# Attention with a gated product and a sparse expert layer: second products three steps behind the first, and announcements of jumps to TensorE alone

## The chip, the cores and the metric

The kernel runs on one core of a Trainium2 chip. The metric is the device time of one execution in microseconds (us); the median of three runs is given. One execution is also recorded by the hardware profiler, and all rows come from that record. The engines are TensorE (PE, matrix products; PEld is its weight load), VectorE (DVE), ScalarE (ACT), GpSimd (POOL) and SyncE (SP, which only issues DMAs here). Each has its own instruction stream; they meet in semaphores.

## The reference

```
# 1: attention, 8 batches, S = 1856, D = 256, 64 score columns
scores = z @ z.T / S;  attn = max(scores, 0) ** 2
x = (u * (attn @ v)).reshape(14848, 256)
# 2: experts, 4 groups of 4, F = 1024
g_idx = argmax(x @ w_group);  e_idx = argmax(xg @ w_expert[g])
h = max(xg @ w1[g, e], 0);  ye = h @ w2[g, e]
out[token] = (softmax weight of group and expert) * ye
```

All in float32. Each of the 14848 rows goes to one of 16 experts.

## The kernel before, in words

**Precision.** Every float32 operand of a product is split into a high and a low part (`hh` and `hl`, `xh` and `xl`, weights `h` and `l`), and a product is three matmuls: low by high, high by high, high by low. The high part is a copy on ScalarE, the low part a subtraction on VectorE.

**Two stages.** Up to about 858 us the attention runs, batch by batch; its result rows are routed and scattered into a bucket in DRAM, sorted by expert. Then comes the expert stage, which the change is about. The experts are ordered by their number of rows. Each has a list of blocks of rows (`PARTS`): 512 + 256 + 512 for the two largest, 384 + 256 + 512 for three more, 512 + 512 for eight, 384 + 512 for two, 512 + 352 for the last. The very first blocks of the two largest are done ahead.

**Steps.** A block takes NF = 8 steps, and `g` counts the steps of all blocks. `body(g)` issues, in this order: `up`, the first product of step g (six matmuls, L767 to L769, into one PSUM bank `ph`; ScalarE reads the bank into `hh`, L771; VectorE reads it into `hl`, L772, after which the bank is free); then `downs(g - AHEAD)`, the second product of an earlier step (six matmuls, L782 to L784, into the two banks `y` of its block); then, at three steps of a block, a piece of `join_block` for the next block (`xf`, `xh`, `xl`); then whatever `then(g, ...)` has put down for this step. Three banks serve `ph` in turn, four serve `y`, and one (`ps_m`) serves the router's small products.

**What hangs on a step.** After the last second product of a block, `turn` copies `y` to `yp` (ScalarE, L812), transposes it by DMA from SyncE into `yr` (L821), and some steps later `rows_out` makes `yf` on VectorE (a copy L827 and a multiply L831 for each half of the block) and scatters it to the output from POOL (L787). Weights come as four pieces of 512 KB an expert: SyncE loads a raw piece (`load_w`, L197, L206) one expert ahead of its cutting, and the cutting (ScalarE L201, L213; VectorE L202, L214) is put on the steps listed in `CUTS`, counted from the end of a region. A piece's next raw load is issued by the main loop after the step that cut it (`owed`). Rows of a coming block are transposed in by SyncE as `xp` (L728), from `more_rows`.

**Versions.** The last block of an expert has a number of rows known only at run time. It is compiled in eight versions, 512 to 288 columns wide; `region(i)` holds them. Each engine jumps by itself into the version that a register names, and jumps out at its end. A version holds the eight steps of its block and the first AHEAD steps of the next. `hint(j, engines)` issues an instruction that announces the coming jump's target to an engine: to TensorE right after the region before, to the other four in step 4 or 5 of the block ahead. There are fifteen such entries. The widths that the record shows, in order: 288, 288, 384, 384, 384, 512, 480, 448, 416, 416, 384, 352, 352, 480, 416. The first five follow a block of 256 rows, the others one of 512 or 384.

**Order.** In the expert stage the order on PE, ACT, DVE and SP is the program's order, as written (`manual_schedule`). An engine that waits holds up everything behind it.

Of the kernel before, what the change touches and what calls it, by code (L numbers as in the profile page):

```python
# [9 lines left out]
F32 = mybir.dt.float32  # L10
# [9 lines left out]
P = 128  # L20
# [11 lines left out]
def tile_glu_attn_moe(  # L32
# [14 lines left out]
    NE, _, F = w1.shape  # L47
    N = B * S
    ND = D // P
# [30 lines left out]
    ps_s = ctx.enter_context(tc.tile_pool(name="ps_s", bufs=3, space=PSUM))  # L80
    ps_o = ctx.enter_context(tc.tile_pool(name="ps_o", bufs=4, space=PSUM))
    ps_m = ctx.enter_context(tc.tile_pool(name="ps_m", bufs=1, space=PSUM))

    def sb(tag, shape, dt, bufs, name):
        return pool.tile(shape, dt, tag=tag, bufs=bufs, name=name)
# [7 lines left out]
    def new_stg(name):  # L93
        return sb("stg", [P, 1024], F32, 2, name)
# [4 lines left out]
    def new_rows(name):  # L99
        return sb("rows", [P, 4, RW], I32, 3, name)  # L100
# [7 lines left out]
    def bank(pl, tag, name):  # L108
        return pl.tile([P, 512], F32, tag=tag, name=name)
# [80 lines left out]
    def load_w(e, wt, piece, name, wide=False):  # L190

        if wide and piece > 1:
            raw = sb("ut", [P, ND, 512], F32, 2, f"raw_{name}_{piece}").rearrange("p d q -> p (d q)")
        else:
            raw = new_stg(f"raw_{name}_{piece}")
        if piece < 2:
            nc.sync.dma_start(raw, w1[ds(e, 1), piece * P:(piece + 1) * P, :].rearrange("o p f -> p (o f)"))  # L197

            def split():
                hi, lo = wt["h"][piece], wt["l"][piece]  # L200
                held(nc.scalar.copy(out=hi, in_=raw))  # L201
                nc.vector.tensor_sub(out=lo, in0=raw, in1=f32(hi))  # L202
        else:
            q = piece - 2
            rv = raw.rearrange("p (a d) -> p a d", d=D)
            nc.sync.dma_start(  # L206
                rv, w2[ds(e, 1), q * 4 * P:(q + 1) * 4 * P, :].rearrange("o (a p) d -> p (o a) d", p=P)
            )

            def split():  # L210
                for j in range(2):
                    t = wt["2"][2 * q + j].rearrange("p (a t d) -> p a t d", a=2, t=2)
                    held(nc.scalar.copy(out=t[:, :, 0, :], in_=rv[:, 2 * j:2 * j + 2, :]))  # L213
                    nc.vector.tensor_sub(out=t[:, :, 1, :], in0=rv[:, 2 * j:2 * j + 2, :], in1=f32(t[:, :, 0, :]))  # L214

        return split
# [123 lines left out]
    ut = {}  # L340
# [362 lines left out]
    dyn = {i for i in range(NB) if blocks[i] == parts[blocks[i][0]][-1] and blocks[i][0] < NDYN}  # L703
# [49 lines left out]
    def join_block(i, given=None):  # L753
# [5 lines left out]
        )  # L759
        yield from join_x(i, xp, n, given)  # L760

    def up(name, wt, x, f, W, given=None):
        xh, xl = x
        fs = slice(f * P, (f + 1) * P)
        o = bank(ps_s, "s", f"ph_{name}_{f}")[:, 0:W]
        for d in range(ND):
            nc.tensor.matmul(o, wt["l"][d][:, fs], xh[:, d, 0:W], start=(d == 0), stop=False)  # L767
            nc.tensor.matmul(o, wt["h"][d][:, fs], xh[:, d, 0:W], start=False, stop=False)  # L768
            nc.tensor.matmul(o, wt["h"][d][:, fs], xl[:, d, 0:W], start=False, stop=(d == ND - 1))  # L769
        hh, hl_ = given or (new_z(f"hh_{name}_{f}"), new_z(f"hl_{name}_{f}"))  # L770
        nc.scalar.activation(out=hh[:, 0:W], in_=o, func=AF.Relu)  # L771
        nc.vector.scalar_tensor_tensor(out=hl_[:, 0:W], in0=o, scalar=0.0, in1=f32(hh[:, 0:W]),  # L772
                                       op0=ALU.max, op1=ALU.subtract)
        return hh, hl_
# [84 lines left out]
    def next_view():  # L859
# [3 lines left out]
    PE, ACT, DVE, SP, POOL = (  # L863
        mybir.EngineType.PE, mybir.EngineType.Activation, mybir.EngineType.DVE, mybir.EngineType.SP, mybir.EngineType.Pool
    )
# [243 lines left out]
        nc.vector.tensor_copy(out=ki, in_=tiles)  # L1109


    AHEAD = 2
    OLD = NB - 1
    xb = {0: xs[0]}
    hb = {}
# [3 lines left out]
    def then(g, fn):  # L1119
        at.setdefault(g, []).append(fn)  # L1120

    CUTS = {2: (0, 6, 9, 13), 3: (0, 4, 6, 9), 4: (0, 2, 4, 8), 5: (0, 2, 4, 8)}
    cuts = {}
    owed = []

# [5 lines left out]
    def weights_from(g):  # L1131

        ld = blocks[g // NF - 1][0] + 2
        if ld >= NE:
            return
        wts[ld].update(new_w(f"e{ld}"))

        def piece(pc):
            cuts[(ld, pc)]()
            owed.append((ld + 1, pc))  # L1140

        for pc, k in enumerate(CUTS.get(ld, (0, 1, 3, 4))):
            then(g + k, lambda pc=pc: piece(pc))

    def downs(g, W=None):
        i, f = divmod(g, NF)
        e, r0, n = blocks[i]
        if f == 0 and i not in yb:
            yb[i] = [bank(ps_o, "o", f"y_{i}_{d}") for d in range(ND)]
        down(wts[e], f, hb.pop(g), yb[i], W or n)  # L1150
        if f == NF - 1:
            fns = turn(i, yb.pop(i), rows_b.pop(i)[1], n, W, ygiven.get(i))
            for k, fn in enumerate(fns):
                then(g + AHEAD + (5 if i in dyn else 8 if i == OLD - 1 else 6) + k, fn)

    ygiven = {}

# [38 lines left out]
    def body(g, W=None, given=None, xgiven=None):  # L1196

        i, f = divmod(g, NF)
        e, r0, n = blocks[i]
        d = (g - AHEAD) // NF  # L1200
        hb[g] = up(i, wts[e], xb[i], f, W if W and i in dyn else n, given)
# [13 lines left out]
    def hint(j, engines):  # L1215
        if j < NDYN:
            tc.switch_hint({eng: to_arm[j] for eng in engines}, NW, f"arm{j}")

    def region(i):

        g0 = i * NF
        yb[i] = [bank(ps_o, "o", f"y_{i}_{d}") for d in range(ND)]
        xgiven = new_xhl(f"m{i + 1}")
        ygiven[i] = [sb("zr", [P, 512], F32, 2, f"yr_{i}_{t0}") for t0 in (0, 2)]
        given = {
            g0 + NF + k: tuple(sb(tag, [P, 512], F32R, n, f"{h}_{i + 1}_{k}") for h in ("hh", "hl"))
            for k, (tag, n) in enumerate((("zm", 2), ("r", 4)))
        }
        held_state = [(x, dict(x)) for x in (hb, yb, xb, rows_b)]
        held_at = {k: list(v) for k, v in at.items()}  # L1230
        views_at = ocnt[0]
        owed_at = list(owed)
        for k in tc.Switch(to_arm[blocks[i][0]], NW, hint=f"arm{blocks[i][0]}"):
            for x, was in held_state:
                x.clear()
                x.update(was)
            at.clear()
            at.update({k_: list(v_) for k_, v_ in held_at.items()})
            ocnt[0] = views_at
            owed[:] = owed_at  # L1240
            for g in range(g0, g0 + NF + AHEAD):
                body(g, WIDE[k], given.get(g), xgiven)
                if g == g0 + NF - 1:
                    del xb[i]
        late["joined"] += 1
# [9 lines left out]
    with order:  # L1255
        g = 0
        while g < NB * NF:
            i, f = divmod(g, NF)
            e, r0, n = blocks[i]
            if f == 0 and i in dyn:  # L1260
                region(i)
                g += NF + AHEAD
                hint(e + 1, (PE,))
                weights_from(g)
                while owed:
                    load_piece(*owed.pop(0))
                more_rows()
                continue
            body(g)
            if i < NEARLY:  # L1270
                early(i)
            if i + 1 == NEARLY and f == 3:
                while deferred or gens:
                    early(i)
                more_rows()
                counts()
                arms()
                overflow_count()
            if i == NEARLY and f == 0:
                for pc in range(4):  # L1280
                    load_piece(NEARLY, pc)
                load_arms()
                hint(0, (PE,))
            while owed:
                load_piece(*owed.pop(0))
            if i + 1 in dyn and f == (4 if n < 3 * P else 5):
                hint(e, (ACT, DVE, SP, POOL))
            if i + 1 < NB and f == (4 if i + 1 == NEARLY else 3) + 2:
                late["joined"] += 1
            if f > 5:  # L1290
                more_rows()
            if f == NF - 1:
                del xb[i]
            g += 1
        after = [fn for k in sorted(at) for fn in at.pop(k)]
        i = NB - 1
        e, r0, n = blocks[i]
        hs = [hb.pop(i * NF + k) for k in range(NF)]
        with tc.manual_schedule(engines={POOL}):
            for fn in after:  # L1300
                fn()
            for t in range((n + P - 1) // P):
                rows_down(i, wts[e], hs, rows_b[i][1], n, t, next_view)
            assert not hb
            overflow()
# [36 lines left out]
```

## Time and profile before

| | us |
|---|---|
| median of three runs (1573.93 to 1580.88) | 1574.33 |
| the profiled execution | 1587.49 |
| its span, first to last instruction | 1585.7 |
| expert stage in it | about 858 to 1577 |
| TensorE busy in the span | 1514.5 |

The profiled execution is 13 us slower than the median; sums over its rows are made against its own 1587.49 us. "Issue" in the chain of waits or ahead of an instruction is time in which an engine waited for nothing that the profile shows; right behind a jump it is the time until the first instruction of the target is there. PEclk is the share of TensorE's clock that was granted.

### The profile page before, as it was taken

What the parts mean: (1) busy time and instruction counts of PE and PEld (TensorE: products, weight loads), DVE (VectorE), ACT (ScalarE), POOL (GpSimd) and SP (SyncE); (2) the same over time, 40 slices, a digit from 0 to 9 for tenths busy, and PEclk for the clock granted to TensorE, in tenths of its full rate; (3) what the DMA queues carried; (4) which work ended last, traced back from release to release, by engine and by line L of the source; (5) the groups of instructions that cost most, each with busy time, mean ns of one, the idle gap of its engine ahead of it and who ended that gap; (6) DMA issues with size and microseconds to landing.
All of it is one profiled execution on the core that took longest, in us unless ns stands there. A gap on an engine that the chain in (4) does not pass through costs nothing.

```text
span 1585.7 us, 24254 instructions
## 1 busy us (share of the span) xinstructions
PE 1514.5 (96%) x7607; PEld 1318.1 (83%) x7607; DVE 1103.6 (70%) x2619; ACT 996.1 (63%) x1885; POOL 297.0 (19%) x343
## 2 busy tenths in 40 slices
PE   9999999999999999999999999999999889889897
PEld 7888888888888888888887888998887778788796
DVE  7788888888787888887986565555555555555463
ACT  8888888888878888887873343444433334343342
POOL 0022121121212121111121212221122122122122
PEclk9999999999999999999999999999999999999999
DMA  5324333333344352325744646664565665455541
GB/s 142 100 82 106 83 82 105 77 105 85 75 101 92 78 113 68 89 70 151 235 116 90 136 105 131 141 121 93 101 123 117 126 122 115 79 117 119 107 84 48
DMA packets 303588, 167.76 MB, mean 106 GB/s; under 512 B 239467, under 2 KB 282477, under 8 KB 303216
## 3 DMA queue, kind: packets, MB, share of 16 engines
q1 hardware_dynamic: 290896, 132.63, 38.5%
q0 software_dynamic: 11968, 30.91, 7.1%
q14 instruction: 277, 2.27, 0.6%
q8 instruction: 95, 1.56, 0.4%
q10 hardware_dynamic: 352, 0.39, 0.1%
HBM read 72.51 MB, written 41.60 MB: 72 GB/s over the span
## 4 chain that ended last, share of the span: by engine, by line
PE 74%; issue 11%; DVE 6%; DMA 3%; ACT 2%; SPq 1%; POOL 1%; DVEq 0%; POOLq 0%; ACTq 0%
PE o L381 12%; PE o L382 12%; PE o L384 11%; PE sc L349 6%; PE sc L350 6%; PE y L784 5%; PE ph L767 4%; PE ph L768 4%; PE ph L769 4%; PE y L782 4%; PE y L783 4%; DVE hl L772 1%; DMA out_dram<-yf,meta 1%; DMA yr<-yp 1%; DVE w_e L214 1%
## 5 line engine op out<-in xcount | busy, mean ns | idle before, releaser
L771 ACT ACTIVATE hh<-ph 128x512 fp32r<-128x512 f32 (+7 forms) x296 | 151.4, 516 | 409.2 <-PE ph L769 345.1
L772 DVE SCALAR_TENSOR_TENSOR hl<-ph,hh 128x512 fp32r<-128x512 f32 (+7 forms) x296 | 169.8, 582 | 310.3 <-ACT hh L771 230.4
L381 PE MATMUL o<-ah,vl 128*128 128x512 f32 (+1 forms) x960 | 354.7, 371 | 0.8 <-DVE ah L359 0.4
L382 PE MATMUL o<-ah,vh 128*128 128x512 f32 (+1 forms) x960 | 354.4, 371 | 0.0
L362 DVE TENSOR_TENSOR al<-r,ah 128x512 fp32r<-128x512 f32 (+1 forms) x448 | 285.4, 638 | 51.7 <-ACT r L356 43.0
L352 ACT ACTIVATE r<-sc 128x512 f32<-128x512 f32 (+1 forms) x480 | 260.5, 553 | 94.1 <-PE sc L350 66.4
L384 PE MATMUL o<-al,vh 128*128 128x512 f32 (+1 forms) x896 | 295.4, 372 | 0.4 <-DVE al L362 0.4
L784 PE MATMUL y<-hl,w_e 128*128 128x512 f32 (+7 forms) x576 | 207.4, 360 | 53.3 <-DVE hl L772 53.3
L787 POOL DMA_INDIRECT out_dram<-yf,meta x129 | 139.7, 1083 | 562.2 <-DVE yf L831 528.6
L358 ACT ACTIVATE r<-r 128x512 f32<-128x512 f32 (+1 forms) x416 | 241.1, 592 | 6.1
L576 POOL DMA_INDIRECT bucket<-rows,di x120 | 133.0, 1108 | 540.9 <-issue 219.2
L767 PE MATMUL ph<-xh_m,w1l_e 128*128 128x512 f32 (+7 forms) x592 | 211.1, 357 | 0.6 <-issue 0.6
L768 PE MATMUL ph<-xh_m,w1h_e 128*128 128x512 f32 (+7 forms) x592 | 210.2, 355 | 0.0
L769 PE MATMUL ph<-xl_m,w1h_e 128*128 128x512 f32 (+7 forms) x592 | 209.8, 354 | 0.0
L782 PE MATMUL y<-hh,w_e 128*128 128x512 f32 (+7 forms) x576 | 204.4, 355 | 3.0 <-ACT hh L771 3.0
L381 PEld LDWEIGHTS o<-ah,vl 128*128 128x128 f32 x960 | 180.5, 188 | 29.5 <-DVE ah L359 0.9
L783 PE MATMUL y<-hh,w_e 128*128 128x512 f32 (+7 forms) x576 | 203.8, 354 | 0.0
L382 PEld LDWEIGHTS o<-ah,vh 128*128 128x128 f32 x960 | 180.5, 188 | 27.3
L359 DVE CAST ah<-r 128x512 fp32r<-128x512 f32 (+1 forms) x416 | 166.1, 400 | 37.2 <-ACT r L358 35.7
L384 PEld LDWEIGHTS o<-al,vh 128*128 128x128 f32 x896 | 165.3, 188 | 27.9 <-DVE al L362 0.9
L349 PE MATMUL sc<-zm,z2h 128*128 128x512 f32 (+1 forms) x480 | 179.9, 375 | 0.0
L350 PE MATMUL sc<-zm,z2l 128*128 128x512 f32 (+1 forms) x480 | 177.7, 371 | 0.0
(148 smaller groups left out, 2080.2 us busy)
## 6 DMA issues: line engine op xcount, KB each, us to landing
raw_e<-in_w_dram SPq DMA_DIRECT2D x64, 512.0 KB, 5.1
ut<-in_uT_dram SPq DMA_DIRECT2D x24, 512.0 KB, 3.8
vr<-in_v_dram SPq DMA_DIRECT2D x23, 512.0 KB, 4.2
bucket<-padrow SPq DMA_DIRECT2D x16, 528.0 KB, 5.0
zr<-in_zT_dram SPq DMA_DIRECT2D x47, 128.0 KB, 3.9
ut<-in_uT_dram SPq DMA_DIRECT2D x8, 320.0 KB, 3.0
vr<-in_v_dram SPq DMA_DIRECT2D x9, 256.0 KB, 2.8
out_dram<-yf,meta POOLq DMA_INDIRECT x129, 5.0
```

Of the source, the lines that this page charges most:

```text
L349: nc.tensor.matmul(ps[:, 0:w], z2h[:, ks], zm, start=True, stop=False)
L350: nc.tensor.matmul(ps[:, 0:w], z2l[:, ks], zm, start=False, stop=True)
L362: nc.vector.tensor_sub(out=al, in0=a, in1=f32(ah))
L381: nc.tensor.matmul(o, vl[:, dsl], ah, start=(k == 0), stop=False)
L382: newest[:] = [nc.tensor.matmul(o, vh[:, dsl], ah, start=False, stop=(k == NK - 1))]
L384: nc.tensor.matmul(o, vh[:, dsl], al, start=False, stop=False)
L767: nc.tensor.matmul(o, wt["l"][d][:, fs], xh[:, d, 0:W], start=(d == 0), stop=False)
L768: nc.tensor.matmul(o, wt["h"][d][:, fs], xh[:, d, 0:W], start=False, stop=False)
L769: nc.tensor.matmul(o, wt["h"][d][:, fs], xl[:, d, 0:W], start=False, stop=(d == ND - 1))
L782: nc.tensor.matmul(o, w2t[:, 1, dsl], hh[:, 0:W], start=(f == 0), stop=False)
L783: nc.tensor.matmul(o, w2t[:, 0, dsl], hh[:, 0:W], start=False, stop=False)
L784: nc.tensor.matmul(o, w2t[:, 0, dsl], hl_[:, 0:W], start=False, stop=(f == NF - 1))
```

## The change

Five things change, all in the expert stage. Second products follow three steps behind the first (`AHEAD = 3`), and so a version holds three steps of the next block, whose `hh` and `hl` get tiles of their own. From the third block on every fourth first product goes into the bank `ps_m`, so that four banks serve in turn. The steps of the weight pieces change: for two-part experts from 0, 1, 3, 4 to 0, 1, 2, 9 after a region, and since the next region begins five steps after the last, the fourth piece is cut inside the next version and its next raw load is issued after that. The second half of a version's own output rows is put four steps after the first. The announcement to ACT, DVE, SP and POOL is left out. Three buffers change place for it: the raw pieces 2 and 3 use the `rows` tiles, the transposed output of a version the `ut` tiles, and `zr` holds the extra pair.

```
-            raw = sb("ut", [P, ND, 512], F32, 2, f"raw_{name}_{piece}").rearrange("p d q -> p (d q)")
+            raw = new_rows(f"raw_{name}_{piece}").rearrange("p a b -> p (a b)")[:, 0:1024].bitcast(F32)
...
+    many = []
+
     def up(name, wt, x, f, W, given=None):
...
-        o = bank(ps_s, "s", f"ph_{name}_{f}")[:, 0:W]
+        o = (bank(ps_m, "m", f"ph_{name}_{f}") if many and f % 4 == 3 else bank(ps_s, "s", f"ph_{name}_{f}"))[:, 0:W]
...
-    AHEAD = 2
+    AHEAD = 3
...
-    CUTS = {2: (0, 6, 9, 13), 3: (0, 4, 6, 9), 4: (0, 2, 4, 8), 5: (0, 2, 4, 8)}
+    CUTS = {2: (0, 7, 9, 12), 3: (0, 4, 6, 9), 4: (0, 2, 4, 8), 5: (0, 2, 4, 8)}
...
-        for pc, k in enumerate(CUTS.get(ld, (0, 1, 3, 4))):
+        for pc, k in enumerate(CUTS.get(ld, (0, 1, 2, 9))):
             then(g + k, lambda pc=pc: piece(pc))
...
-                then(g + AHEAD + (5 if i in dyn else 8 if i == OLD - 1 else 6) + k, fn)
+                then(g + AHEAD + (4 + 4 * k if i in dyn else (8 if i == OLD - 1 else 6) + k), fn)
...
-        ygiven[i] = [sb("zr", [P, 512], F32, 2, f"yr_{i}_{t0}") for t0 in (0, 2)]
+        yr = sb("ut", [P, ND, 512], F32, 2, f"yr_{i}")
+        ygiven[i] = [yr[:, k] for k in range(2)]
...
-            for k, (tag, n) in enumerate((("zm", 2), ("r", 4)))
+            for k, (tag, n) in enumerate((("zm", 2), ("zr", 2), ("r", 4)))
...
             if i == NEARLY and f == 0:
+                many.append(True)
...
-            if i + 1 in dyn and f == (4 if n < 3 * P else 5):
-                hint(e, (ACT, DVE, SP, POOL))
```

## The prediction

> **What bounds the kernel now.** I read the page first: busy shares, the chain, the costliest groups.
>
> ```profile
> span 1585.7 us, 24254 instructions
> PE 1514.5 (96%) x7607; PEld 1318.1 (83%) x7607; DVE 1103.6 (70%) x2619; ACT 996.1 (63%) x1885; POOL 297.0 (19%) x343
> PE 74%; issue 11%; DVE 6%; DMA 3%; ACT 2%; SPq 1%; POOL 1%; DVEq 0%; POOLq 0%; ACTq 0%
> L784 PE MATMUL y<-hl,w_e 128*128 128x512 f32 (+7 forms) x576 | 207.4, 360 | 53.3 <-DVE hl L772 53.3
> ```
>
> TensorE is the bound, but 11% of the chain is "issue" (an engine that waits for nothing the profile shows), and one group alone idles TensorE for long: the third matmul of a second product, 53.3 us, waiting for `hl` of VectorE. Next I cut the expert stage at the fifteen entries into a version and asked for busy time and granted clock of each stretch. Width minus "PE busy" is the stall at that entry; PEclk is the column after the POOL one.
>
> ```profile
> 887.00:905.00 18.00, 14.81 (x101) 14.35 (x101) 8.36 (x16) 4.88 (x12) 3.94 (x4) 0.91 0.61 93
> 916.00:934.00 18.00, 14.21 (x93) 13.98 (x92) 10.44 (x18) 7.04 (x16) 4.04 (x4) 0.81 0.50 102
> 965.00:983.00 18.00, 14.25 (x74) 13.61 (x74) 6.31 (x12) 4.32 (x9) 2.96 (x3) 0.81 0.61 114
> 1014.00:1032.00 18.00, 14.83 (x96) 14.36 (x96) 8.19 (x15) 5.86 (x13) 2.96 (x3) 1.00 0.67 114
> 1063.00:1081.00 18.00, 14.61 (x87) 14.10 (x86) 7.92 (x14) 5.12 (x12) 2.95 (x3) 0.91 0.82 138
> 1106.00:1124.00 18.00, 18.00 (x82) 14.89 (x81) 9.87 (x15) 7.13 (x13) 4.68 (x4) 1.00 1.00 197
> 1152.00:1170.00 18.00, 16.41 (x76) 13.77 (x75) 7.54 (x13) 6.11 (x11) 4.39 (x4) 1.00 0.87 170
> 1197.00:1215.00 18.00, 14.08 (x60) 12.25 (x59) 6.04 (x11) 5.16 (x10) 3.84 (x4) 0.91 0.81 155
> 1244.00:1262.00 18.00, 12.70 (x58) 11.67 (x57) 5.67 (x10) 3.81 (x8) 4.17 (x4) 0.91 0.87 167
> 1291.00:1311.00 20.00, 13.25 (x53) 12.12 (x52) 5.76 (x10) 4.02 (x8) 4.07 (x4) 0.74 0.80 156
> 1341.00:1361.00 20.00, 12.61 (x59) 11.76 (x58) 5.37 (x11) 4.57 (x10) 3.76 (x4) 0.83 0.84 140
> 1388.00:1406.00 18.00, 13.95 (x71) 13.04 (x70) 6.77 (x12) 5.47 (x11) 4.68 (x4) 0.91 0.76 161
> 1431.00:1449.00 18.00, 14.86 (x69) 13.95 (x68) 6.66 (x13) 5.08 (x11) 4.67 (x4) 0.81 0.79 163
> 1472.00:1490.00 18.00, 11.25 (x48) 9.64 (x47) 6.67 (x12) 3.90 (x8) 4.55 (x4) 0.81 0.91 167
> 1517.00:1535.00 18.00, 18.00 (x97) 17.40 (x96) 11.12 (x18) 6.13 (x14) 4.54 (x4) 1.00 0.46 84
> sum 274.00, PE 217.82 PEld 200.88 DVE 112.70 ACT 78.58 POOL 60.20; mean PE 14.52 PEld 13.39 DVE 7.51 ACT 5.24 POOL 4.01
> ```
>
> So the stalls are 274.0 - 217.8 = 56.2 us, all of them at entries. After most of them the clock is low for a while: (1 - PEclk) times the width adds up to 30 us; the low stretch begins inside the stall, so I count three quarters of it (an estimate), 23 us. What can be won is 56 + 23 = 79 us.
>
> Why an entry stalls stands in the chain around two of them (the fifth and the tenth), and in the timeline of the tenth by engine: TensorE, ScalarE, VectorE, then the DMA queue of SyncE, with the landing of its last transposes (view of the tile `yr` there).
>
> ```profile
> 1062.89 4.85 DMA yr<-yp
> 1067.86 0.77 DVE yf L827
> 1068.95 5.16 issue
> 1074.20 0.57 DVE hl L772
> ...
> 1292.91 10.73 issue
> 1303.73 0.60 DVE hl L772
> ```
>
> ```profile
> 1291.01 0.35 PE L767 MATMUL ph<-xh_m,w1l_e 128*128 128x416 f32 x1
> 1292.13 0.39 PE L782 MATMUL y<-hh,w_e 128*128 128x512 f32 x1
> 1293.49 0.35 PE L767 MATMUL ph<-xh_m,w1l_e 128*128 128x416 f32 x1
> 1304.38 0.72 PE L784 MATMUL y<-hl,w_e 128*128 128x416 f32 x1 [6.75 <-DVE hl L772]
> 1294.49 0.93 ACT L771 ACTIVATE hh<-ph 128x416 fp32r<-128x416 f32 x2 [4.04 <-issue]
> 1303.73 1.59 DVE L772 SCALAR_TENSOR_TENSOR hl<-ph,hh 128x416 fp32r<-128x416 f32 x3 [10.43 <-issue]
> 1288.88 1.16 SPq L197 DMA_DIRECT2D raw_e<-in_w_dram  x2
> 1291.87 8.23 SPq L728 DMA_TRANSPOSE xp<-bucket  x1
> 1307.09 5.16 SPq L821 DMA_TRANSPOSE yr<-yp  x4
> DMA to landing us min/median/max: 2.4/2.5/2.5
> ```
>
> TensorE enters the version at 1291.01 without a gap. VectorE jumps at 1292.91, although announced, and has no instruction for 10.73 us; its `hl` of the version's first step comes at 1303.73, and the second product of that step at 1304.38. ScalarE's jump cost 4.04 us: it came soon after the weight loads began (1288.88), VectorE's came 4 us into them. So a jump costs 4 to 5 us in itself and up to 11 in the traffic of the four loads. [...]
>
> **The change, part by part.** *One step more, and the fourth bank.* A second product now follows its first by three steps, and the first product three steps on no longer waits for the bank that `hl` frees. Both limits move by one step, so TensorE covers one first product of the version plus one second product of the block before. By the rows, six matmuls take 1292.13 - 1291.01 = 1.12 us at 416 columns and 1293.49 - 1292.13 = 1.36 at 512; scaled by columns, a step is 1.5 to 1.7 us at the first five entries (256-column blocks ahead), and 2.3 to 2.65 at the eight later ones that stall. Entry by entry, never below zero, the 56.2 us become 30 (9 in the first five, 21 in the others: 1.4, 2.8, 4.3, 5.0, 1.7, 0.8, 4.4). Alone this saves 26 us of stall; low clock would stay after the four from 2.8 us up, some 8 of the 23.
>
> *Output rows leave the way to the jump.* At the second to fifth entry the chain goes through `yf`: transposes, copy, multiply, then the jump. `yf` of the block two before moves from the step before the jump to the version's first step, and the second half of a version's own `yf` from the step before the next jump to that version's third step. Each half costs VectorE this, and a piece of cut weights this (groups of VectorE between exit and entry):
>
> ```profile
> L214 DVE TENSOR_TENSOR w_e<-raw_e,w_e 128x512 fp32r<-128x512 f32 x4 | 2.6, 685 | 0.0
> L827 DVE COPY yf<-yr 128x1024 uint16<-128x1024 uint16 x2 | 1.5, 744 | 0.0
> L831 DVE TENSOR_TENSOR yf<-yf,meta 128x512 f32<-128x512 f32 x2 | 1.4, 692 | 0.1
> ```
>
> So 744 + 692 ns = 1.4 us ahead of the jump goes, plus the wait for the transposes at the early entries. Their remainder after the first part (about 2 us each) falls to 0.3 each. POOL's two scatters of the moved half go behind POOL's jump; nothing waits for them but buffers that come round ten steps later. Cost nothing.
>
> *The fourth weight piece moves into the version.* Between exit and entry VectorE loses 1.4 us (two L214) and 1.4 of `yf` and one `hl`, 3.4 in all, while the interval loses one step, 2.7 us: its jump comes some 0.7 to 1 us sooner against TensorE. SyncE leaves the version one step later, so its three loads start near 1291.4 to 1292 instead of 1288.9 (1.5 MB instead of 2 MB); the fourth is issued at the exit, 5 us sooner, ahead of the next `xp` transpose. VectorE's jump, near 1292, then stands to the loads as ScalarE's did: I take 4 to 5 us for 10.4 (ends: 4 and 11). Its `hl` is there near 1297; TensorE, which stalled from 1304.38 - 6.75 = 1297.6 on, would stall from 1297.6 + 2.5 = 1300.1 on, 9 us after the entry. So the eight later entries stall no more. Inside the version the moved work (1.4 + 1.4 of VectorE, 1.2 of ScalarE) lies in a stretch where VectorE is busy 5.8 of 20 us. If that cover were gone it would cost 2.8 us in each of eight versions.
>
> *Announcements to ScalarE, VectorE, SyncE and POOL go.* They did not save the jumps above; only entries six and fifteen came without stall. Bounds: nothing, or one more fetch of 4 to 11 us a jump. I take nothing, nearest to the announced jumps that cost 4 to 11 all the same; what is added up to 3 us a jump lies under the new cover.
>
> *What is late next.* The transposes of the block before (L821) start at 1307.09, when SyncE has got through `xp` and its own jump; this hardly moves. Their `yf` is due on VectorE at the version's ninth step, whose `hl` without the stall comes some 20 us after the entry at 416 columns and 18 at 352 (the matmuls above, plus 1.5 us for ScalarE and VectorE); the first pair lands near 1310.9 (the second of four 1.3 us issues, at 1308.4, plus 2.5), 20 us after the entry. VectorE waits up to 2 us there in narrow versions, leaves them later and jumps later next time: I put 2 us on three entries, 6 in all.
>
> The sum, against this execution's 1587.5 us: 79 to win, less 1.7 (first entry, 3.19 - 1.5), 1.2 (the four after it), 6 (narrow entries) and 3.4 of low clock that remains: 67 saved, 1520. The median of the runs is 13 us lower than this execution; half of that may be jumps that are slower only when profiled, so I take 60 off the median: 1574.3 - 60 = 1514.
>
> **The clock.** A stall of 3.17 us (fourth entry) left PEclk at 1.00, one of 3.14 (thirteenth) at 0.81. [...]
>
> **The rivals.**
> *Cover alone* (jumps cost VectorE as long as now, since loads and jump move together): 26 of stall and 15 of clock saved, 41, with the allowance for the profiled run in proportion 37: 1537. For it: SyncE's place is estimated, and the loads need slip only 2 us. Against: three loads, and a step later.
> *VectorE waits for the transposes.* If SyncE gets later by one `xp` (8.23 us in traffic), VectorE stands 5 to 8 us at step nine of a version, beyond the 7 us of cover with its 4 us exit jump: 3 us of stall a version in thirteen, 40 with some clock, of the 60: 1554. Against: the four transposes end at 1312.25, the version's own follow its last step, 26 us after the entry at 416 columns (1317): there is room.
> *Unannounced jumps cost more: slower.* If an unannounced jump takes two fetches in a row, VectorE's are 10 us at the early entries (twice 5.16) and, with the loads, 10 to 21 at the eight later ones (twice 5.16, twice 10.73), 16 in the middle. With 9 us of cover and a jump 1 us after the entry that is 8 to 9 us of stall in eight and 4 in five, 90 for 56, with clock 35 for 23: about 1620. It decides from some 13 us a jump. Against: the announcements bought nothing visible. [...]
> *It does nothing:* the stall follows the version's arrival, not the cover, 1574.
>
> **How the numbers follow.** Forecast 0.47 (own range 1497 to 1530), cover alone 0.25 (to 1548), transposes 0.12 (1545 to 1568), unannounced 0.08, nothing 0.08 (half of it within 0.5%, about what a measurement of this kernel tells from no change). Range 1495 (all 79 saved) to 1552. Faster 0.84, same 0.06, slower 0.10.
>
> **What would show it.** Right: the L784 group waits under 15 us; PEclk near 1.00 in the entry stretches; VectorE's `hl` at an entry idle 4 to 6 us on issue. Cover alone: L784 near 30 and issue rows still 8 to 11. Transposes: `yf` L827 waiting for `yr`. Unannounced: issue rows on ScalarE and VectorE above 12 us. I would be wrong above all if SyncE's loads still start before VectorE's jump by several us, or if the longer version stalls TensorE itself at the jump.

## The result, and the profile after

The changed kernel takes 1507.08 us (median of four executions, 1505.53 to 1508.2) against 1575.29 (1573.93 to 1580.88): ratio 0.956, 95% interval 0.9534 to 0.9586. The forecast was 1514, faster. The profiled execution of after takes 1506.0 us (span 1504.2), that of before 1587.49.

First the page of after: span, busy shares, the chain by engine, and the group that carried the stalls (the third matmul of a second product, L784 before, L786 now). Lines from 762 on have moved down by two.

```profile
span 1504.2 us, 23839 instructions
PE 1488.0 (99%) x7607; PEld 1297.4 (86%) x7607; DVE 1102.7 (73%) x2619; ACT 996.0 (66%) x1885; POOL 298.6 (20%) x343
PE 39%; issue 2%; DMA 1%; DVE 1%; ACT 0%; POOL 0%; POOLq 0%; DVEq 0%; ACTq 0%
L786 PE MATMUL y<-hl,w_e 128*128 128x512 f32 (+7 forms) x576 | 200.5, 348 | 0.4 <-DVE hl L774 0.4
```

TensorE is busy for 99% of the span; "issue" fell from 11% of the chain to 2%, and 53.3 us of waiting for `hl` became 0.4. What TensorE still waits for in the expert stage (total, times, longest) is next to nothing:

```profile
PE ph L769 <- issue: 1.3, 2, 0.7
PE y L786 <- DVE hl L774: 0.4, 1, 0.4
PE ph L771 <- DVE xl_m L750: 0.2, 1, 0.2
```

The fifteen entries, cut as before (width, then PE busy; PEclk after the POOL column): the first, fourth, tenth and fifteenth, and the sum.

```profile
887.00:905.00 18.00, 17.41 (x132) 16.76 (x130) 9.94 (x21) 6.39 (x16) 6.28 (x7) 1.00 0.60 96
...
998.00:1016.00 18.00, 17.61 (x113) 17.30 (x112) 9.71 (x18) 5.92 (x13) 3.88 (x4) 1.00 0.59 105
...
1248.00:1266.00 18.00, 18.00 (x93) 17.04 (x92) 12.78 (x21) 8.15 (x15) 4.98 (x4) 1.00 0.80 204
...
1435.00:1453.00 18.00, 17.99 (x98) 17.57 (x97) 12.29 (x21) 7.86 (x16) 4.63 (x4) 1.00 0.67 130
sum 270.00, PE 268.16 PEld 250.92 DVE 167.69 ACT 113.41 POOL 73.72; mean PE 17.88 PEld 16.73 DVE 11.18 ACT 7.56 POOL 4.91
```

The stall at entries is 270.0 - 268.2 = 1.8 us for 56.2, and PEclk is 1.00 in all fifteen. This accounts for the saving between the two profiled executions: 56.2 - 1.8 = 54.4 us of stall, and 1514.5 - 1488.0 = 26.5 us of busy time of the same 7607 matmuls, which goes with the clock (mean granted share 0.978 before, 0.998 after); together 80.9 of 81.5.

The timeline of the tenth entry, for TensorE, ScalarE, VectorE and the queue of SyncE:

```profile
1249.29 0.35 PE L769 MATMUL ph<-xh_m,w1l_e 128*128 128x416 f32 x1
1258.23 0.35 PE L786 MATMUL y<-hl,w_e 128*128 128x416 f32 x1
1253.14 0.93 ACT L773 ACTIVATE hh<-ph 128x416 fp32r<-128x416 f32 x2 [4.29 <-PE ph L771]
1251.14 0.68 DVE L774 SCALAR_TENSOR_TENSOR hl<-ph,hh 128x512 fp32r<-128x512 f32 x1
1253.69 1.09 DVE L774 SCALAR_TENSOR_TENSOR hl<-ph,hh 128x416 fp32r<-128x416 f32 x2 [1.87 <-ACT hh L773]
1245.66 0.40 SPq L206 DMA_DIRECT2D raw_e<-in_w_dram  x1
1252.07 0.96 SPq L197 DMA_DIRECT2D raw_e<-in_w_dram  x2
1253.23 0.38 SPq L206 DMA_DIRECT2D raw_e<-in_w_dram  x1
1263.29 1.22 SPq L823 DMA_TRANSPOSE yr<-yp  x1
```

TensorE enters at 1249.29. The version's first `hl` is there 4.4 us later (before: 12.7 us), and its consumer runs at 1258.23, 8.9 us after the entry, without a wait. Three of the four raw loads start only 2.8 us after the entry. ScalarE's row ends its idle time "<-PE ph", though `ph` was done long before: that is its jump, of which this view shows no other sign.

**Reading a jump.** The idle column hides a jump as soon as a semaphore fires meanwhile. So I also took, from the records of the branch and of the first instruction behind it, when VectorE jumps and how long it then has nothing; R is TensorE's first matmul of the version. Means over entries 7 to 14, us:

| kernel | jump at | jump takes | first `hl` at |
|---|---|---|---|
| before | R + 2.2 | 8.5 | R + 10.8 |
| after | R + 0.4 | 3.8 | R + 4.7 |

In after ScalarE's jump ends about as late as VectorE's: it starts at R - 0.8 and takes 4.5 us (means), and at six of these eight entries (all but the twelfth and the fourteenth) `hh` is finished after VectorE's jump has ended, so that the first `hl` waits for ScalarE. A still earlier jump of VectorE alone would bring `hl` little sooner.

At 416 columns TensorE needs this `hl` 6.6 us after R with two steps between the products (1297.6 against 1291.01 in the prediction's rows), and 8.9 with three.

### The profile page after: what moved, and what is told of

Same layout as the page of the kernel before. It is cut to its first block, busy times and chain, and to the rows that moved or that the text cites. A ratio compares the mean times of both kernels' runs of the same rounds, so it can differ in the third digit from the quotient of the medians.

```text
span 1504.2 us, 23839 instructions
## 1 busy us (share of the span) xinstructions
PE 1488.0 (99%) x7607; PEld 1297.4 (86%) x7607; DVE 1102.7 (73%) x2619; ACT 996.0 (66%) x1885; POOL 298.6 (20%) x343
## 5 line engine op out<-in xcount | busy, mean ns | idle before, releaser
L789 POOL DMA_INDIRECT out_dram<-yf,meta x129 | 144.1, 1117 | 458.3 <-DVE yf L833 411.7
L769 PE MATMUL ph<-xh_m,w1l_e 128*128 128x512 f32 (+7 forms) x592 | 205.5, 347 | 1.3 <-issue 1.3
L771 PE MATMUL ph<-xl_m,w1h_e 128*128 128x512 f32 (+7 forms) x592 | 205.5, 347 | 0.3 <-DVE xl_m L750 0.2
L770 PE MATMUL ph<-xh_m,w1h_e 128*128 128x512 f32 (+7 forms) x592 | 205.1, 346 | 0.0
L786 PE MATMUL y<-hl,w_e 128*128 128x512 f32 (+7 forms) x576 | 200.5, 348 | 0.4 <-DVE hl L774 0.4
L784 PE MATMUL y<-hh,w_e 128*128 128x512 f32 (+7 forms) x576 | 200.1, 347 | 0.0
L785 PE MATMUL y<-hh,w_e 128*128 128x512 f32 (+7 forms) x576 | 200.0, 347 | 0.0
```

The costliest lines, as they stand in the source:

```text
L784: nc.tensor.matmul(o, w2t[:, 1, dsl], hh[:, 0:W], start=(f == 0), stop=False)
L785: nc.tensor.matmul(o, w2t[:, 0, dsl], hh[:, 0:W], start=False, stop=False)
L786: nc.tensor.matmul(o, w2t[:, 0, dsl], hl_[:, 0:W], start=False, stop=(f == NF - 1))
```

## The experiments

All were timed against the kernel before, whose medians in these four comparisons were 1575.84, 1576.29, 1576.17 and 1571.85. "Steps" is the distance of the products. "Early" rows are the output rows ahead of the first versions (blocks of 256 rows in front), "later" ones the second half of a version's own rows; yes means behind the next jump. The intervals reach 6 to 11 us either way, so differences of a few us between two kernels are not settled by them.

| kernel | steps | banks | early, later rows moved | fourth piece late | median | ratio (95%) | third `y` matmul waits | jump at, takes; `hl` at |
|---|---|---|---|---|---|---|---|---|
| e2_no_hints | 2 | 3 | no, no | no | 1582.35 | 1.0029 (0.9991 to 1.0067) | 44.2 | takes 7.0 |
| e7_light_loads | 2 | 3 | no, no | no | 1526.96 | 0.9687 (0.9631 to 0.9743) | 12.5 | 2.2, 3.4; 5.7 |
| e11_loads_later | 2 | 3 | no, no | no | 1537.36 | 0.9765 (0.9699 to 0.9832) | 16.6 | 2.2, 4.3; 6.6 |
| e10_rows_three_banks | 2 | 3 | yes, yes | no | 1519.87 | 0.9663 (0.9603 to 0.9724) | 9.5 | 0.0, 6.6; 6.8 |
| e9_rows_alone | 2 | 4 | yes, yes | no | 1522.25 | 0.9669 (0.9595 to 0.9742) | 7.4 | 0.0, 6.1; 6.3 |
| e8_placing_alone | 2 | 4 | yes, yes | yes | 1517.99 | 0.9629 (0.9561 to 0.9698) | 8.7 | 0.0, 4.4; 4.4 |
| e6_two_ahead | 2 | 4 | no, yes | yes | 1531.5 | 0.9712 (0.9657 to 0.9767) | 15.4 | -0.1, 4.6; 4.6 |
| e4_cover_alone | 3 | 4 | yes, no | no | 1525.52 | 0.9674 (0.9623 to 0.9724) | 9.3 | 2.4, 5.3; 7.7 |
| e3_loads_ahead | 3 | 4 | yes, yes | no | 1510.83 | 0.9581 (0.9532 to 0.9631) | 0.0 | 1.0, 4.2; 5.3 |
| e5_three_banks | 3 | 3 | yes, yes | yes | 1514.46 | 0.9607 (0.9551 to 0.9663) | 0.0 | 0.8, 3.7; 5.1 |
| e1_hints_back | 3 | 4 | yes, yes | yes | 1509.47 | 0.9568 (0.952 to 0.9616) | 0.7 | 0.7, 3.6; 4.8 |

### The announcements (e1, e2)

e1 is after with the announcement put back; e2 is before with these two lines taken out:

```
             if i + 1 in dyn and f == (4 if n < 3 * P else 5):
                 hint(e, (ACT, DVE, SP, POOL))
```

> The changed kernel with the announcement to ScalarE, VectorE, SyncE and POOL put back. Theory (announcements to these four buy nothing): 1507 us within 6, the first product's ScalarE wait on issue at an entry stays 4 to 5 us. Rival (an announcement saves a fetch): jumps of 1 us or less on ScalarE, but since the stalls are gone already the time stays within 6 of 1507. Rival (an announcement costs, because it takes a fetch of its own in the stretch ahead): 1512 or more, with new waits ahead of entries.

> The kernel before with the announcement to ScalarE, VectorE, SyncE and POOL left out, nothing else. Here the jumps lie on the path, so their price shows. Theory (they buy nothing): 1575 within 8, VectorE's issue rows 4 to 11 us as before. Rival (an unannounced jump costs one fetch more, 4 to 11 us): ten or more stalls longer by 4 us or more, 1620 or above. Rival (announcing costs): 1565 or less.

Neither moves the time: e1 takes 1509.47, with an interval that overlaps that of after, e2 1.0029 with an interval that holds 1. The waits of TensorE in e2 are those of before in kind:

```profile
PE y L784 <- DVE hl L772: 44.2, 15, 5.4
```

VectorE's jumps average 7.0 us without the announcement, 8.5 with it, and 3.6 with it in e1 against 3.8 in after. Dropping it costs nothing that these runs can show.

It is not quite without effect, though. In the four kernels that announce (before, e1, e7, e11) 6 of the 168 jumps of ScalarE, VectorE and SyncE into a version other than that of 512 columns took under 1 us, and one took 1.1, such as 0.42 us on ScalarE at the eleventh entry of e1 and 0.54 on VectorE at the ninth of e11. In the nine kernels that do not, none of 378 took under 2 us. So an announcement seems to make a jump short now and then, too rarely to show in the time; why it mostly does not is open.

### The fourth weight piece (e3)

```
-        for pc, k in enumerate(CUTS.get(ld, (0, 1, 2, 9))):
+        for pc, k in enumerate(CUTS.get(ld, (0, 1, 3, 4))):
```

> The changed kernel with the weight pieces of two-part experts at steps 0, 1, 3, 4 after a region, as before, so that the fourth piece is cut and loaded again ahead of the jump. Theory (the place of the loads against the jump made the difference): SyncE now issues four loads around the jump, VectorE's jump takes 7 to 11 us again at the later entries, the third matmul of the second product waits 10 to 20 us in all, 1520 to 1540. Rival (one more step of cover was enough by itself): waits under 5 us, 1507 to 1514.

Measured 1510.83, some 4 us above after: far less than the theory said, and in the range of its rival. Queue of SyncE and first `hl` of the tenth version, which TensorE enters at 1252.86:

```profile
1252.66 0.95 SPq L197 DMA_DIRECT2D raw_e<-in_w_dram  x2
1254.27 1.28 SPq L206 DMA_DIRECT2D raw_e<-in_w_dram  x1
1259.17 1.58 DVE L774 SCALAR_TENSOR_TENSOR hl<-ph,hh 128x416 fp32r<-128x416 f32 x3 [4.22 <-issue]
```

The loads start at R - 0.2 with the old steps too, where before they started at R - 2.1 (1288.88 against 1291.01). So the late piece is not needed to hold the loads back that far: the longer version does it, since it holds one step more and SyncE leaves it later. The late piece holds them back further. As means over entries 7 to 14, the first of the loads of `w1` (L197) starts at R - 2.2 with two steps and the old pieces (e9), at R + 0.6 here and at R + 2.4 in after; against VectorE's jump that is 2.2 us ahead, 0.3 ahead and 2.0 behind. The jump itself is nearly as short here as in after, 4.2 us for 3.8, and the cutting of the late piece, 1.3 us of VectorE, moves to an uncritical place (jump at R + 0.4 for R + 1.0).

### The second half of a version's rows put back (e4)

e3 and, besides:

```
-                then(g + AHEAD + (4 + 4 * k if i in dyn else (8 if i == OLD - 1 else 6) + k), fn)
+                then(g + AHEAD + (4 + k if i in dyn else (8 if i == OLD - 1 else 6) + k), fn)
```

> The changed kernel with the weight pieces at 0, 1, 3, 4 and both halves of a version's output rows ahead of the next jump, as before: three steps and four banks remain, and the announcements stay out. Theory (cover is worth 26 us of stall and 15 of clock, the rest is placing): 1530 to 1545, VectorE's jump 8 to 11 us at the later entries. Rival (cover is all): 1507 to 1514. Rival (placing is all, cover gives nothing): 1560 or more.

1525.52 us, below the range that I gave: the jumps do not stay at 8 to 11 us, since with the loads at R + 1.6 (tenth entry) VectorE still jumps early in them. But they start 1.4 us later (R + 2.4 for R + 1.0), and `hl` comes at R + 7.7 on average, at the twelfth to fourteenth entry at R + 8.9 to 11.4, where TensorE stalls again:

```profile
PE y L786 <- DVE hl L774: 9.3, 6, 3.1
```

(Of the six waits, 3.1 us fall on the second entry, 6.0 on the twelfth to fifteenth.) Against e3 these rows cost 15 us, for 1.4 us of VectorE ahead of a jump: stalls return, and low clock with them (mean clock 0.994 for 0.997).

### The fourth bank (e5)

After without the line `many.append(True)`.

> The changed kernel without the fourth bank: first products take three banks in turn. A first product then waits for the subtraction three steps back, so TensorE's cover after an entry is the old one. Theory (placing does most: ScalarE and VectorE jump together, ahead of the loads, and their work is there 5 to 6 us after the entry, before TensorE wants it at 6.5): stalls of 0 to 1.5 us an entry, now on the first product's first matmul, 1507 to 1520. Rival (the extra step of cover does most): 2 to 3 us at each of thirteen entries with low clock after some, 1535 or more.

1514.46, 7 us above after (1512.48 to 1517.76 for 1505.53 to 1508.2). The stall moves to the first product, which waits for its bank:

```profile
PE ph L769 <- DVE hl L774: 5.7, 7, 2.0
```

With three steps between the products the bank is needed: 5.7 us of waits in seven places, 5.4 of them in the first five versions.

### Two steps, the rest as in after (e6, then e8)

e6 is after with `AHEAD = 2`, no `zr` pair, and the steps counted so that every piece and half stays where it is (`(0, 1, 2, 10)`, `5 + 4 * k`), but the early rows fall ahead of the jump, as before. e8 is e6 with those moved too:

```
-                then(g + AHEAD + (5 + 4 * k if i in dyn else (8 if i == OLD - 1 else 6) + k), fn)
+                then(g + AHEAD + (5 + 4 * k if i in dyn else (8 if i == OLD - 1 else 7) + k), fn)
```

> The changed kernel with second products two steps behind again, and the placing kept: the fourth piece on the fifth step of the next version, the second half of the output rows on its third step; four banks, no announcements but TensorE's. SyncE leaves a version a step earlier against the next entry, so its loads start some 2.5 us sooner. Theory (placing does most): stalls of 1 to 3 us an entry, 1515 to 1535. Rival (cover does most): 1545 or more. Rival (placing does all): 1507 within 6.

> Second products two steps behind as in the kernel before, with the late fourth piece, four banks and no announcement; the output rows of blocks ahead of a version also move to the version's first steps, so that no yf stands ahead of VectorE's jump at the early entries. With the rows ahead of the jump the same kernel took 1531.5 us, all its 15.4 us of waiting of the third y matmul at the early entries. If the placing of VectorE's work is the cause (theory), these waits fall to under 5 us and the time to 1508-1516 us; the third step of cover is then not needed. If the cover is what counts there (rival), the waits stay at 10 us or more and the time at 1524-1532 us.

Waits of TensorE, e6 and then e8:

```profile
PE y L786 <- DVE hl L774: 15.4, 6, 4.8
```

```profile
PE y L786 <- DVE hl L774: 8.7, 8, 3.1
PE y L784 <- ACT hh L773: 2.9, 3, 2.1
```

In e6 15.1 of the 15.4 us fall on the early entries: at seven of the eight later ones `hl` is there 4.1 to 4.6 us after the entry, ahead of the need at 6.6, without the third step. In e8 the waits for `hl` at the early entries fall from 15.1 to 2.0 us, so there the rows ahead of the jump were the cause. The total still misses the theory's 5 us, and 1517.99 its range by 2 us, since two other waits came up: 3.1 us between two entries (at 1402) and 2.9 at the fourteenth, whose `hl` comes at R + 8.8. With the first entry (2.1 us for `hh` and 1.0 for `hl`) they add up to 9 us, about the 11 that lie between e8 and after.

### Only the output rows moved (e9, e10)

e9 is e8 with the pieces at `(0, 1, 3, 4)`; e10 is e9 without the fourth bank. So e10 differs from before by the moved rows, the buffers that this takes, the cut steps of one expert (0, 7, 9, 12 for 0, 6, 9, 13), and the announcements (worth nothing by e2).

> The same with the weight pieces at their old steps (0, 1, 3, 4 after a region): only the output rows are moved, second products stay two steps behind, so SyncE's four raw loads start ahead of VectorE's jump as in the kernel before. If those loads in flight during VectorE's jump set the stalls of the eight later entries (theory), its jumps there take 6-11 us again, the third y matmul waits 15-30 us and the time is 1535-1555 us. If the output rows ahead of the jump were all that mattered (rival), the jumps take 4-5 us and the time is 1508-1518 us.

> Second products two steps behind, weight pieces at their old steps, three banks, no announcement: against the kernel before only the output rows are moved behind the jumps (and the buffers changed for it). The same with a fourth bank took 1522 us. With two steps between the products a second product meets a late hl ahead of the bank's next first product, so by theory the fourth bank is worth nothing here: 1516-1528 us, the third y matmul waiting 5-12 us in all. If the bank counts as it did with three steps (7 us), 1529 us or more and a wait of the first ph matmul for hl appears.

e9 takes 1522.25 and e10 1519.87: no difference, so the fourth bank is worth nothing at two steps, as expected, and the rows alone give 52 of the 68 us (1571.85 - 1519.87). On e9 both of my expectations failed: the jumps are longer than in e8, as the theory had it (6.1 us for 4.4), but they cause little stall. The profiled execution of e10 took 1528.9 us, 9 above its median, so its waits are on the high side. Waits of TensorE in e10, then the tenth entry of e10 (TensorE's entry, first `hl`, loads):

```profile
PE y L786 <- DVE hl L774: 9.5, 6, 4.4
PE y L784 <- ACT hh L773: 4.3, 3, 2.6
```

```profile
1257.17 0.35 PE L769 MATMUL ph<-xh_m,w1l_e 128*128 128x416 f32 x1
1264.52 1.09 DVE L774 SCALAR_TENSOR_TENSOR hl<-ph,hh 128x416 fp32r<-128x416 f32 x2 [6.46 <-ACT hh L773]
1254.61 1.15 SPq L197 DMA_DIRECT2D raw_e<-in_w_dram  x2
1255.96 1.02 SPq L206 DMA_DIRECT2D raw_e<-in_w_dram  x2
```

The loads start at R - 2.6, as early as before. But with no `yf` in front VectorE jumps 0.2 us before R instead of 1.9 after it, 2.3 us into the loads instead of 4.0, and its jump takes 6.4 us instead of 10.8: it ends at R + 6.1, and the `hl` at R + 7.4 instead of R + 12.7. (The last 1.2 us are ScalarE's: its jump takes 7.4 us at this entry, and the row names `hh`; at the seven others VectorE's jump ends last or within 0.1 us of `hh`.) Over the eight entries the `hl` comes 4.0 us sooner, 2.2 of it by jumping sooner and 1.9 by a shorter jump. With the need at 6.6 this takes away nearly all that went beyond it.

### The loads in flight (e7, e11)

e7 is before with an eighth of each raw weight piece loaded from the third expert on, and that eighth used in place of the rest; seven eighths of these weights are left out. e11 is before with the raw loads held back until the last `xp` ahead of the jump is issued:

```
-            while owed:
-                load_piece(*owed.pop(0))
             if i + 1 in dyn and f == (4 if n < 3 * P else 5):
...
                 more_rows()
+            while owed and f == NF - 1:
+                load_piece(*owed.pop(0))
```

> The kernel before with an eighth of each raw weight piece loaded and used eight times in the cut (from the third expert on); this leaves out seven eighths of those weights, the instructions on every engine stay. Theory (a jump's length is its fetch, held up by the traffic of the loads): VectorE's issue rows at the later entries fall from 6 to 11 us to 4 to 5, ScalarE's stay 3 to 5, stalls fall by 20 to 30 us plus clock: 1530 to 1550. Rival (the length has another cause, such as the widths' place in memory): rows as before, 1575 within 8.

> The kernel before, with SyncE's raw loads of the next expert held back until after the last xp transpose ahead of the jump (some 5 to 8 us later); VectorE's order is unchanged, its output rows stand ahead of the jump. If the loads in flight are what makes VectorE's jumps long (theory), its jumps at the eight later entries take 4-6 us instead of 6-11, and of their 40 us of stall some 10-20 are left: 1535-1555 us. If the place of the output rows alone counts (rival), the jumps stay at 6-11 us and the time within 1565-1580 us.

In both VectorE jumps at R + 2.2, as in before. With light loads the jump takes 3.4 us for 8.5, with later ones 4.3 (4.8 without the announced jump of 0.54); the times are 1526.96 and 1537.36. The first lies 3 us below the range that the theory gave, the second in it, and both far from their rivals'. ScalarE's jumps, which the theory of e7 left at 3 to 5 us, fell from 3.8 to 2.4: they gain from the light loads too. Waits in e7 (whose lines stand some 17 further down), then in e11, then e11's tenth entry, which TensorE enters at 1265.13:

```profile
PE y L801 <- DVE hl L789: 12.5, 9, 3.0
```

```profile
PE y L784 <- DVE hl L772: 16.6, 11, 2.8
```

```profile
1266.72 0.72 SPq L197 DMA_DIRECT2D raw_e<-in_w_dram  x2
1267.69 1.29 SPq L206 DMA_DIRECT2D raw_e<-in_w_dram  x2
1271.57 1.58 DVE L772 SCALAR_TENSOR_TENSOR hl<-ph,hh 128x416 fp32r<-128x416 f32 x3 [4.14 <-ACT yp L812]
```

So the traffic of the loads is what stretches a jump from some 4 us to 8.5, shown twice by different edits: less of it (3.4 us), and the same amount later (4.3). How the traffic does so is not shown: that a jump's length is a fetch, as the theory of e7 and the rivals about announcements have it, was the author's assumption. The traces have DMA packets of the kind "instruction", five in VectorE's jump of 10.7 us at the tenth entry of before and three in that of 2.8 us in after, but not for which engine they are.

The other kernels line up with it. The table gives, as means over entries 7 to 14, how long before VectorE's jump the first load of `w1` starts (the loads are the full ones in all of these), and how long the jump takes:

| | before | e2 | e10 | e9 | e4 | e11 | e8 | e6 | e3 | after | e1 | e5 |
|---|---|---|---|---|---|---|---|---|---|---|---|---|
| loads ahead of the jump by, us | 4.8 | 4.8 | 2.4 | 2.2 | 1.4 | 1.2 | 0.8 | 0.7 | 0.3 | -2.0 | -2.2 | -2.2 |
| jump takes, us | 8.5 | 7.0 | 6.6 | 6.1 | 5.3 | 4.3 | 4.4 | 4.6 | 4.2 | 3.8 | 3.6 | 3.7 |

So the jump lengthens with its depth in the loads, and not with where the output rows stand as such: e11 has them ahead of the jump as in before.

## Why the prediction was right, step by step

**What bounds it, and how much there is to win: right.** I put 56.2 us of stall and 23 of clock; 54.4 and 26.5 went.

**The residue: wrong, small.** I left 12 us of the 79 standing; of the stalls 1.8 us remain and PEclk is 1.00 at all fifteen entries (the 3.4 us of low clock among the 12 stood on no row), so 81.5 us went between the profiled executions, not 67. The 6 us of VectorE waiting for transposes are 1.8 us in two places:

```profile
L829 DVE COPY yf<-yr 128x1024 uint16<-128x1024 uint16 (+1 forms) x67 | 49.4, 737 | 1.8 <-DMA yr<-yp 1.8
```

I had said that SyncE's transposes hardly move. They start 14.0 us after the entry (1263.29), for 16.1 before: SyncE's own jump averages 2.8 us at entries 7 to 14 for 5.7. Thinner traffic is a likely reason (the DMA engines are busy for 0.3 to 0.6 of the time in these jumps, before for 0.7 to 0.8), but no run here separates it. The first entry's 1.7 us went as well.

**From the profiled time to the median: half right.** I took 60 off the median for 67 in the profile; it was 68 for 81.5. The profiled execution of before stood 12 us above its median. That these were stall too is likely, not shown: the slower executions of before have the lower clock (1587.84 us at a mean of 0.974, 1561.43 at 0.988). The kernel with stalling entries varies more: before ran from 1561.43 to 1587.84, after only from 1505.53 to 1508.2.

**One step more and the fourth bank: mis-sized as a part alone.** I gave it 26 us of stall and 15 of clock, the largest term. It cannot be had quite alone, since the longer version by itself delays SyncE's loads and puts the early rows behind the jump; with only that (e4) the kernel takes 1525.5, where the rival of cover alone said 1537, because its premise (loads and jump move together, so that jumps cost as much as before) is false: they take 5.3 us for 8.5. On top of the moved rows the step is worth 11 us (e8 to after, and e9 to e3 with the pieces as before, four banks in each), and step, bank and late piece together 13 (e10 to after); with three steps, leaving out the bank costs 7.

**Output rows out of the way: the term most undersized.** I let about 2 us fall to 0.3 at four early entries, some 7 us in all, and folded the rest into "0.7 to 1 us sooner". e10 gives 52 us for them. What I missed is that the two causes work together: a jump 2.2 us sooner is also 2 us less deep in the loads (2.4 us for 4.8), and so it is shorter (6.6 us for 8.5).

**The loads behind the jump: mechanism right, one cause taken for the only one.** VectorE's jumps fell to 3.8 us (I took 4 to 5), and its `hl` to R + 4.7 (I had R + 6). The loads start later than I put them, at R + 2.4 for R + 0.4 to R + 1. But the fourth piece, under which I booked this, is not the only way: with three steps the longer version, which I named as a reason for SyncE's lateness, is enough without it (e3), and with two steps the piece alone shortens the jump, 6.1 us to 4.4 (e9 to e8). Nor is it needed for most of the gain: at the eight later entries either moved rows (e10: `hl` at R + 6.8) or later loads (e11: R + 6.6) bring `hl` down to about the need; both together (e6, e8) to R + 4.5, with two steps.

**Announcements at nothing: right** for the time (e1, e2). The slower rival, which took an unannounced jump at twice the measured 5.16 and 10.73 us, is out: VectorE's jumps are 2.8 to 6.3 us in after, but for the sixth, at 0.5.

**The parts do not add up.** Rows 52, later loads 35 (e11), step, bank and placing 11 to 15 on top: each removes the same stalls, and 68 is all there is. That the forecast came within 7 us owes more to this cap, which the first reading had right, than to how I divided it among the parts; there some luck is in it.

Not separated: how the 52 us of e10 divide between the five early entries and the others (e6 against e8 gives 13.5 for the early rows, with loads already late), and why VectorE's jumps in e2 are shorter than in before.

## What to carry over

Where an engine jumps, work put behind the jump instead of ahead of it can be worth more than its own duration, since it sets when the jump begins and how deep in other traffic that falls: in e10 VectorE jumps 2.2 us sooner, its jump takes 6.6 us for 8.5, and its result is there 4.0 us sooner. Cover is best set against one number, here the time from TensorE's entry to the first `hl` against the steps that stand before its use; past the need, more cover buys nothing. Parts of a change that remove the same stall should be priced as alternatives first and only what is left over added.

## What the runs showed of the hardware

- VectorE's jump into a version takes 2.8 to 4.5 us where the main loads start only behind it (by 0.5 to 3.2 us, entries 7 to 14 of after) and 6.2 to 11.3 with four loads of 512 KB issued ahead of it (the same entries of before); with loads an eighth as large at the same place, 2.8 to 4.0.
- The sixth entry goes to the version of 512 columns, the first of the eight in the program: its jump takes 0.5 us on VectorE in every kernel here. Why it is so short, no run shows.
- Announced jumps of ScalarE, VectorE and SyncE took about as long as unannounced ones: over the fifteen entries 66, 59 and 44 us in e1 with, 63, 61 and 49 in after without. Of the 168 announced ones outside the sixth entry (four kernels) 7 were short, 0.3 to 1.1 us; of 378 unannounced ones (nine kernels) none took under 2 us.
